# Token-run x loads, taps as shifts by 32 columns, GELU in store order: a causal convolution and an MLP on one core

## The chip, the cores and the metric

The kernel runs on one core of a Trainium2 chip. The metric is the device time of one execution in microseconds, and each median below is over several executions on one chip. The batches of experiments ran on different chips, each with the kernel before beside it, so a run is compared with the kernel before of its own batch. The span in the profile is 1.7 to 2.2 us shorter than the time of the same execution.

Names: PE is the TensorE matmul, PEld its weight load, DVE is VectorE, ACT is ScalarE, POOL is GpSimd, SP is SyncE. SPq, POOLq and ACTq are the queues on which these engines request DMAs. A load lands when its completion is signalled; an eviction is DVE's copy of a result out of the matmul's buffer; a beat is the time from one GELU tile to the next. The granted clock is the share of TensorE's full speed that the throttle allowed, by the profile's records.

## The reference, cut to what matters

```python
# x: (8, 4096, 192) fp32, weight: (8 heads, 7 taps), w_in: (192, 2048), w_out: (2048, 192)
w = softmax(weight, axis=-1)
x_pad = concat([zeros(B, 6, 192), x], axis=1)          # causal: 6 tokens of halo
out[b, s, h, :] = sum_k w[h, k] * x_pad[b, s + k, head h]
h = out.reshape(32768, 192) @ w_in
y = gelu_exact(h) @ w_out                              # (32768, 192) fp32
```

## The kernel before

The 32768 tokens are cut into two halves that are worked on side by side, on partitions 0 to 63 and 64 to 127. A block is 512 tokens of each half; the first two blocks are half blocks of 256. For each block, DVE transposes x (three STREAM_TRANSPOSE instructions) and runs 21 tap instructions (7 taps, 3 channel groups); PE multiplies by w_in, ACT applies GELU, PE multiplies by w_out, DVE evicts, SP stores. DVE works one block ahead of PE.

```python
WS = [256, 256] + [512] * ((HALF - 512) // 512)
# POOL: weights requested at once, w_in's second part for one half of the partitions only
for hf in range(2):
    g.dma_start(win[first 512 columns], ...).then_inc(S_WIN[0], 16)
...   # build the head selector
g.dma_start(win[columns 512..2047], ...).then_inc(S_WIN[1], 16)
g.dma_start(wout, ...).then_inc(S_WOUT, 16)
for n in range(1, NB):          # halo: the last 6 tokens of the block before
    ...
    g.tensor_copy(dst, ap(xT[(n - 1) % 2], WS[n - 1], [[NP * XW, 128], [XW, NP], [1, HL]]))
# DVE: tap k reads xT shifted by k columns
src = ap(xT[n % 2], p * XW + k, [[NP * XW, 128], [1, w]])
# SP: x in pieces of 160 floats (640 bytes), one piece for each token
ap(xt, off, [[D, 32], [32 * D, w // 32], [1, XC]])
# SP at the start
load(0)
sp.wait_ge(S_XIN[0], 64)
load(1)
sp.wait_ge(S_WIN[1], 16)
sp.dma_start(win[other partitions], win[...])   # copy of w_in's second part inside SBUF
load(2)
for n in range(1, NB + 1):
    if n + 2 < NB: load(n + 2)
    if n >= 2: store(n - 2, 1)
    store(n - 1, 0)             # each block is stored in two halves
store(NB - 1, 1)
```

I call the x of blocks 0, 1, 2 and 3 x0, x1, x2 and x3.

## Time and profile before

The median is 704.16 us in the first three runs.

| quantity | value | read from |
|---|---|---|
| PE busy from 60 to 690 us | 100%, clock 1.00 | table of stretches |
| one GELU tile on PE (two matmul phases) | 1.31 us | timeline |
| GELU on ACT | 1.024 us | groups |
| first matmul of block 2 | 43.66 us | timeline |
| end of the last eviction to the end of the span | 3.0 us | timeline |

The first view is the timeline of the start-up: start, duration, engine, line, operation and, in brackets, the idle time before it and what ended that. A merged row such as the x requests shows its first start and its total extent.

```profile
0.81 10.27 SPq L406 DMA_DIRECT2D xin<-in_x_dram  x8
4.30 0.65 POOL L146 DMA_DIRECT2D win<-in_moe_w_in_dram  x1
9.35 1.10 DVE L193 STREAM_TRANSPOSE xT<-xin 128x256 f32<-128x256 f32 x3 [3.34 <-DMA xin<-in_x_dram]
12.07 0.70 SPq L431 DMA_DIRECT2D win<-win  x1
12.81 13.91 SPq L406 DMA_DIRECT2D xin<-in_x_dram  x8
28.38 1.90 DVE L193 STREAM_TRANSPOSE xT<-xin 128x512 f32<-128x512 f32 x3 [0.40 <-DMA xin<-in_x_dram]
30.32 1.28 DVE L214 TENSOR_SCALAR acc<-xT,wcol 128x512 f32<-128x512 f32 x3
43.66 0.82 PE L333 MATMUL hp<-xc,win 64*128 64x512 bf16 x6 [4.02 <-DVE xc L221]
```

DVE starts when x0 has landed (9.35 us) and waits only 0.40 us for x2 at 28.38 us. PE starts block 2 at 43.66 us, held by DVE's taps. From then on PE sets the pace, so a delay at this point is a delay of the whole kernel, to within about 2 us: in the twelve kernels of the table further down, the stretch from this matmul to the end of the last eviction took 654.9 to 657.5 us.

The table of stretches: window and length, busy time and count of PE, PEld, DVE, ACT and POOL, granted clock, DMA share, GB/s. The DMA share is the mean busy share of the 16 DMA engines; packets that overlap on one engine make it exceed 1.

```profile
7.00:13.00 6.00, 0.00 (x0) 0.00 (x0) 3.62 (x11) 0.00 (x0) 0.20 (x1) 1.00 1.24 192
13.00:19.00 6.00, 0.39 (x5) 0.35 (x7) 5.66 (x15) 0.00 (x0) 0.00 (x0) 1.00 1.24 234
19.00:25.00 6.00, 5.92 (x59) 4.06 (x54) 5.96 (x17) 3.85 (x4) 0.31 (x1) 1.00 1.18 198
```

DVE, once it has x0, waits only 0.34 and 0.40 us for x.

The groups of instructions by shape (total busy us, mean ns, idle before, releaser), before:

```profile
L289 ACT ACTIVATE gT<-hp 128x1024 bf16<-128x1024 f32 x512 | 523.6, 1024 | 161.2 <-PE hp L333 161.2
L214 DVE TENSOR_SCALAR acc<-xT,wcol 128x512 f32<-128x512 f32 x93 | 39.6, 482 | 1.1
L162 POOL COPY xT<-xT 128x18 f32<-128x18 f32 x29 | 12.6, 436 | 567.9 <-DVE xT L193 567.9
```

The middle of the kernel in the view of stretches, and the end of the timeline; the span is 702.9 us:

```profile
60.00:690.00 630.00, 630.00 (x10615) 480.59 (x10612) 497.43 (x817) 493.52 (x482) 11.58 (x28) 1.00 0.47 98
```

```profile
689.38 10.93 SPq L418 DMA_DIRECT2D out_dram<-osb  x3
699.35 0.56 DVE L230 COPY osb<-ob 128x384 f32<-128x384 f32 x1 [0.76 <-PE ob L365]
```

### The profile page before, as it was taken

What the parts mean: (1) busy time and instruction counts of PE and PEld (TensorE: products, weight loads), DVE (VectorE), ACT (ScalarE), POOL (GpSimd) and SP (SyncE); (2) the same over time, 40 slices, a digit from 0 to 9 for tenths busy, and PEclk for the clock granted to TensorE, in tenths of its full rate; (3) what the DMA queues carried; (4) which work ended last, traced back from release to release, by engine and by line L of the source; (5) the groups of instructions that cost most, each with busy time, mean ns of one, the idle gap of its engine ahead of it and who ended that gap; (6) DMA issues with size and microseconds to landing.
All of it is one profiled execution on the core that took longest, in us unless ns stands there. A gap on an engine that the chain in (4) does not pass through costs nothing.

```text
span 702.9 us, 24699 instructions
## 1 busy us (share of the span) xinstructions
PE 676.9 (96%) x11366; PEld 518.1 (74%) x11366; DVE 550.2 (78%) x925; ACT 526.5 (75%) x516; POOL 17.9 (3%) x44
## 2 busy tenths in 40 slices
PE   0879999999999999999999999999999999999997
PEld 0657777777777777777777777777777777777777
DVE  5999778977777977777987777887777897777711
ACT  1669777777777777777777777777777777777771
POOL 2000000000000000000000000000000000000000
PEclk9999999999999999999999999999999999999999
DMA  9945555335555335555434555434565533551012
GB/s 183 177 92 106 123 115 101 84 81 108 123 121 98 91 79 99 122 121 99 101 84 82 122 122 100 108 83 75 121 123 115 100 86 79 108 121 48 24 47 70
DMA packets 104487, 71.05 MB, mean 101 GB/s; under 512 B 5312, under 2 KB 104000, under 8 KB 104384
## 3 DMA queue, kind: packets, MB, share of 16 engines
q1 hardware_dynamic: 101680, 67.71, 46.3%
q0 software_dynamic: 2688, 1.77, 1.8%
q8 instruction: 89, 1.46, 0.9%
q14 instruction: 14, 0.11, 0.1%
q10 hardware_dynamic: 16, 0.00, 0.0%
HBM read 45.48 MB, written 25.17 MB: 101 GB/s over the span
## 4 chain that ended last, share of the span: by engine, by line
PE 93%; DMA 3%; DVE 2%; SPq 0%; issue 0%; POOL 0%; POOLq 0%
PE ob L365 47%; PE hp L333 46%; DMA xin<-in_x_dram 2%; DVE acc L221 1%; DMA win<-in_moe_w_in_dram 1%; SPq L406 0%; POOL win L117 0%; DVE xT L193 0%; DVE acc L214 0%; DVE xc L221 0%; SPq L431 0%; DVE osb L230 0%; POOL sel L124 0%; POOL sel L134 0%; POOL sel L121 0%
## 5 line engine op out<-in xcount | busy, mean ns | idle before, releaser
L289 ACT ACTIVATE gT<-hp 128x1024 bf16<-128x1024 f32 x512 | 523.6, 1024 | 161.2 <-PE hp L333 161.2
L365 PEld LDWEIGHTS ob<-wout,gT 64*128 64x128 bf16 x8192 | 368.9, 94 | 103.2 <-issue 0.7
L333 PE MATMUL hp<-xc,win 64*128 64x512 bf16 (+1 forms) x3168 | 426.9, 373 | 18.1 <-DVE xc L221 16.8
L365 PE MATMUL ob<-wout,gT 64*128 64x192 bf16 x8192 | 428.9, 243 | 0.0
L221 DVE SCALAR_TENSOR_TENSOR acc<-xT,wcol,acc 128x512 f32<-128x512 f32 (+1 forms) x495 | 327.4, 730 | 0.0
L333 PEld LDWEIGHTS hp<-xc,win 64*128 64x128 bf16 x3168 | 163.1, 95 | 73.4 <-issue 18.5
L230 DVE COPY osb<-ob 128x384 f32<-128x384 f32 x128 | 71.0, 556 | 139.3 <-PE ob L365 139.3
L221 DVE SCALAR_TENSOR_TENSOR xc<-xT,wcol,acc 128x512 bf16<-128x512 f32 (+1 forms) x99 | 66.8, 730 | 0.0
L193 DVE STREAM_TRANSPOSE xT<-xin 128x512 f32<-128x512 f32 (+1 forms) x99 | 60.8, 665 | 4.1 <-DMA xin<-in_x_dram 4.1
L214 DVE TENSOR_SCALAR acc<-xT,wcol 128x512 f32<-128x512 f32 (+1 forms) x99 | 41.4, 474 | 1.2
L162 POOL COPY xT<-xT 128x18 f32<-128x18 f32 x29 | 12.6, 436 | 567.9 <-DVE xT L193 567.9
L304 PE MATMUL ob<-wnm,sel 8*128 8x7 f32 x6 | 1.4, 358 | 4.4 <-POOL sel L134 4.4
L304 PEld LDWEIGHTS ob<-wnm,sel 8*128 8x128 f32 x6 | 1.3, 320 | 4.4 <-POOL sel L134 4.4
L274 ACT ACT_TABLE_LOAD x1 | 1.3, 1283 | 1.4 <-PEq L458 1.4
L170 DVE TENSOR_REDUCE wmx<-wsb 8x1 f32<-8x7 f32 x1 | 0.1, 148 | 2.2 <-DMA wsb<-in_weight_dram 2.2
L182 DVE COPY wcol<-ob 128x21 f32<-128x21 f32 x1 | 0.2, 181 | 2.1 <-PE ob L304 2.1
L159 POOL MEMSET xT<- 128x18 f32 x3 | 0.3, 115 | 41.9 <-DVE xc L221 41.9
L117 POOL DMA_DIRECT2D win<-in_moe_w_in_dram x2 | 1.4, 688 | 0.8 <-POOLq L458 0.8
L289 ACT ACT_TABLE_LOAD x1 | 1.3, 1283 | 0.0
L150 POOL DMA_DIRECT2D wout<-in_moe_w_out_dram x1 | 1.2, 1194 | 0.0
L174 DVE TENSOR_SCALAR wsm<-wsm 8x1 f32<-8x1 f32 x1 | 0.1, 142 | 0.8 <-ACT wex L274 0.8
L146 POOL DMA_DIRECT2D win<-in_moe_w_in_dram x1 | 0.6, 647 | 0.0
(12 smaller groups left out, 2.8 us busy)
## 6 DMA issues: line engine op xcount, KB each, us to landing
xin<-in_x_dram SPq DMA_DIRECT2D x124, 320.0 KB, 6.6
out_dram<-osb SPq DMA_DIRECT2D x62, 384.0 KB, 3.0
xin<-in_x_dram SPq DMA_DIRECT2D x8, 160.0 KB, 6.1
wout<-in_moe_w_out_dram POOLq DMA_DIRECT2D x1, 768.0 KB, 17.1
out_dram<-osb SPq DMA_DIRECT2D x4, 192.0 KB, 5.0
win<-in_moe_w_in_dram POOLq DMA_DIRECT2D x1, 576.0 KB, 7.7
win<-win SPq DMA_DIRECT2D x1, 576.0 KB, 9.2
win<-in_moe_w_in_dram POOLq DMA_DIRECT2D x2, 192.0 KB, 6.1
```

Source lines behind the costliest of these rows:

```text
L117: g.dma_start(ap(win, 64 * hf * NP * F, [[NP * F, 64], [F, NP], [1, FC]]), ap(wint, 0, [[F, 64], [64 * F, NP], [1, FC]]),).then_inc(S_WIN[ ...
L150: g.dma_start(ap(wout, 0, [[NF * C, 128], [C, NF], [1, C]]), ap(woutt, 0, [[C, 128], [128 * C, NF], [1, C]]),).then_inc(S_WOUT, 16)
L162: g.tensor_copy(dst, ap(xT[(n - 1) % 2], WS[n - 1], [[NP * XW, 128], [XW, NP], [1, HL]]),).then_inc(S_HALO)
L193: v.transpose(ap(xT[n % 2], p * XW + HL, [[NP * XW, 128], [1, w]]), ap(xin[n % NX], 64 * p, [[TB // 32 * XC, 128], [XC, w // 32], [1, 32]] ...
L214: ins = v.tensor_scalar(a, src, wk, None, ALU.mult)
L221: ins = v.scalar_tensor_tensor(dst, src, wk, a, op0=ALU.mult, op1=ALU.add)
L230: v.tensor_copy(ap(osb[m % 2], 2 * g * C, [[8 * C, 128], [C, 2], [1, C]]), ap(ob[(G0[m] + g) % 2], 0, [[1024, 128], [512, 2], [1, C]]),).t ...
L274: a.activation(out=wex[:, :], in_=wsb[:, :], func=AF.Exp, bias=wmx[:, 0:1], accum_out=wsm[:, 0:1],).then_inc(S_ACTP)
L289: a.activation(out=ap(gT[n % 2], i * c * 2 * w, [[NF * 2 * TB, 128], [w, 2], [2 * w, c], [1, w]],), in_=hp[u % 2][:, :], func=AF.Gelu,).th ...
L304: ins = t.matmul(ob[0][:, p * KS : (p + 1) * KS], sel[:, p * 128 : (p + 1) * 128], wnm[:, :],)
L333: ins = t.matmul(hp[u % 2][:, hf * TB + cc * w : hf * TB + cc * w + w], win[r, p * F + f0 : p * F + f0 + 128], xc[n % 2][r, p * TB : p * T ...
L365: ins = t.matmul(ob[gg % 2][:, 512 * sub : 512 * sub + C], gT[m % 2][r, c0 : c0 + 128], wout[r, i * C : (i + 1) * C], start=(ph == 0 and i ...
```

## The change

The intent is that each partition holds a run of 16 consecutive tokens. One load descriptor is then 12 KB instead of 640 bytes. After the transpose, neighbouring tokens lie 32 columns apart, so a tap is a shift by 32 columns. The halo is no longer 6 columns but 6 x 32: 31 of each 32 columns are copied from the same block, on GpSimd (558 elements per partition), and one of 32 from the block before. GELU writes its output in an order in which each partition of the result holds 4 consecutive tokens, so a store descriptor is 3 KB instead of 768 bytes. The change also holds the weights back until x0 and x1 have landed, and stores a block whole with four DMAs.

```diff
-    HL = KS - 1
+    HB = KS - 1
+    HL = 32 * HB
...
-            for hf in range(2):                      # w_in, first part, at once
-                g.dma_start(... ).then_inc(S_WIN[0], 16)
             g.memset(sel[:, :], 1.0).then_inc(S_SEL)
...
+            def halo(n):
+                ...   # 18 elements from the block before (or zeros)
+                g.wait_ge(S_TR, NP * (n + 1))
+                g.tensor_copy(
+                    ap(xT[n % 2], 1, [[NP * XW, 128], [XW, NP], [32, HB], [1, 31]]),
+                    ap(xT[n % 2], WS[n], [[NP * XW, 128], [XW, NP], [32, HB], [1, 31]]),
+                ).then_inc(S_HALO)
+            g.wait_ge(S_XIN[0], 64)
+            for hf in range(2):
+                g.dma_start(... ).then_inc(S_WIN[0], 16)
+            halo(0)
+            g.wait_ge(S_XIN[1], 64)
             g.dma_start(...).then_inc(S_WIN[1], 16)  # w_in, second part
             g.dma_start(...).then_inc(S_WOUT, 16)
...
-                    v.wait_ge(S_HALO, n + 1)
+                if k == 1 and p == 0:
+                    v.wait_ge(S_HALO, 2 * n + 2)
...
-                src = ap(xT[n % 2], p * XW + k, [[NP * XW, 128], [1, w]])
+                src = ap(xT[n % 2], p * XW + 32 * kt, [[NP * XW, 128], [1, w]])
...
+                    if c == 1:
+                        src = [[2 * TB, 128], [w // 4, 8], [32, w // 128], [1, 32]]
+                        dst = [[NF * 2 * TB, 128], [32, 8], [256, w // 128], [1, 32]]
...
-                        ap(xt, off, [[D, 32], [32 * D, w // 32], [1, XC]]),
+                        ap(xt, off, [[mb * D, 32], [1, mb * D - 32]]),
...
-                if n >= 2:
-                    store(n - 2, 1)
-                store(n - 1, 0)
-            store(NB - 1, 1)
+                store(n - 1)                          # whole, four DMAs
```

More of the change, by code (lines that the diff above doesn't have):

```diff
@@ L37, in bass_lightweight_conv__then__act_gelu_exact_kernel @@
     assert NF == 16
-    XC = 160
-    HL = KS - 1
+    HB = KS - 1
+    HL = 32 * HB
     XW = HL + TB
@@ L55, in bass_lightweight_conv__then__act_gelu_exact_kernel @@
     G0 = [sum(NG[:n]) for n in range(NB + 1)]
+    OUTS = []
+    for n in range(NB):
+        OUTS.append((64 if NCH[n] == 1 else 128) + (OUTS[n - 2] if n >= 2 else 0))
     es = ExitStack()
@@ L81, in bass_lightweight_conv__then__act_gelu_exact_kernel @@
         wcol = sbt("wcol", [128, NP * KS], F32)
-        xin = [sbt("xin%d" % i, [128, TB // 32 * XC], F32) for i in range(NX)]
+        xin = [sbt("xin%d" % i, [128, TB // 32 * D], F32) for i in range(NX)]
         xT = [sbt("xT%d" % i, [128, NP * XW], F32) for i in range(2)]
@@ L115, in _ @@
         def _(g):
-            for hf in range(2):
-                g.dma_start(
-                    ap(win, 64 * hf * NP * F, [[NP * F, 64], [F, NP], [1, FC]]),
-                    ap(wint, 0, [[F, 64], [64 * F, NP], [1, FC]]),
-                ).then_inc(S_WIN[0], 16)
             g.memset(sel[:, :], 1.0).then_inc(S_SEL)
@@ L142, in _ @@
             ).then_inc(S_SEL)
-            halo_memset = ap(xT[0], 0, [[NP * XW, 128], [XW, NP], [1, HL]])
-            g.memset(halo_memset, 0.0).then_inc(S_HALO)
+            def halo(n):
+                dst = ap(xT[n % 2], 0, [[NP * XW, 128], [XW, NP], [32, HB]])
+                if n >= 2:
+                    g.wait_ge(S_CV, NCV * (n - 1))
+                if OFF[n] % SEQ == 0:
+                    g.memset(dst, 0.0).then_inc(S_HALO)
+                else:
+                    g.wait_ge(S_TR, NP * n)
+                    g.tensor_copy(
+                        dst,
+                        ap(
+                            xT[(n - 1) % 2],
+                            WS[n - 1] + 31,
+                            [[NP * XW, 128], [XW, NP], [32, HB]],
+                        ),
+                    ).then_inc(S_HALO)
+                g.wait_ge(S_TR, NP * (n + 1))
+                g.tensor_copy(
+                    ap(xT[n % 2], 1, [[NP * XW, 128], [XW, NP], [32, HB], [1, 31]]),
+                    ap(xT[n % 2], WS[n], [[NP * XW, 128], [XW, NP], [32, HB], [1, 31]]),
+                ).then_inc(S_HALO)
+            g.wait_ge(S_XIN[0], 64)
+            for hf in range(2):
+                g.dma_start(
+                    ap(win, 64 * hf * NP * F, [[NP * F, 64], [F, NP], [1, FC]]),
+                    ap(wint, 0, [[F, 64], [64 * F, NP], [1, FC]]),
+                ).then_inc(S_WIN[0], 16)
+            halo(0)
+            g.wait_ge(S_XIN[1], 64)
             g.dma_start(
@@ L154, in _ @@
             for n in range(1, NB):
-                dst = ap(xT[n % 2], 0, [[NP * XW, 128], [XW, NP], [1, HL]])
-                if n >= 2:
-                    g.wait_ge(S_CV, NCV * (n - 1))
-                if OFF[n] % SEQ == 0:
-                    g.memset(dst, 0.0).then_inc(S_HALO)
-                else:
-                    g.wait_ge(S_TR, NP * n)
-                    g.tensor_copy(
-                        dst,
-                        ap(xT[(n - 1) % 2], WS[n - 1], [[NP * XW, 128], [XW, NP], [1, HL]]),
-                    ).then_inc(S_HALO)
+                halo(n)
         @block.vector
@@ L191, in trans @@
                     if n >= 1:
-                        v.wait_ge(S_HALO, n)
+                        v.wait_ge(S_HALO, 2 * n)
                 v.transpose(
@@ L197, in trans @@
                         64 * p,
-                        [[TB // 32 * XC, 128], [XC, w // 32], [1, 32]],
+                        [[TB // 32 * D, 128], [D, w // 32], [1, 32]],
                     ),
@@ L205, in conv @@
                     v.wait_ge(S_TR, NP * (n + 1))
-                    v.wait_ge(S_HALO, n + 1)
+                if k == 1 and p == 0:
+                    v.wait_ge(S_HALO, 2 * n + 2)
                 idx = NCV * n + NP * k + p
+                kt = KS - 1 - k
                 if idx >= NP:
                     v.wait_ge(S_CV, idx - NP + 1)
-                src = ap(xT[n % 2], p * XW + k, [[NP * XW, 128], [1, w]])
-                wk = wcol[:, p * KS + k : p * KS + k + 1]
+                src = ap(xT[n % 2], p * XW + 32 * kt, [[NP * XW, 128], [1, w]])
+                wk = wcol[:, p * KS + kt : p * KS + kt + 1]
                 a = acc[:, p * TB : p * TB + w]
@@ L228, in evac @@
                 if m >= 2 and g == 0:
-                    v.wait_ge(S_OUT[m % 2], 32 * (m // 2))
+                    v.wait_ge(S_OUT[m % 2], OUTS[m - 2])
                 v.tensor_copy(
-                    ap(osb[m % 2], 2 * g * C, [[8 * C, 128], [C, 2], [1, C]]),
+                    ap(osb[m % 2], g * C, [[8 * C, 128], [4 * C, 2], [1, C]]),
                     ap(ob[(G0[m] + g) % 2], 0, [[1024, 128], [512, 2], [1, C]]),
@@ L288, in _ @@
                         a.wait_ge(S_MM2, G0[n - 1])
-                    a.activation(
-                        out=ap(
-                            gT[n % 2],
-                            i * c * 2 * w,
-                            [[NF * 2 * TB, 128], [w, 2], [2 * w, c], [1, w]],
-                        ),
-                        in_=hp[u % 2][:, :],
+                    if c == 1:
+                        src = [[2 * TB, 128], [w // 4, 8], [32, w // 128], [1, 32]]
+                        dst = [[NF * 2 * TB, 128], [32, 8], [256, w // 128], [1, 32]]
+                    else:
+                        src = [[2 * TB, 128], [TB, 2], [128, 4], [1, 128]]
+                        dst = [[NF * 2 * TB, 128], [128, 2], [256, 4], [1, 128]]
+                    a.activation(
+                        out=ap(gT[n % 2], i * c * 2 * w, dst),
+                        in_=ap(hp[u % 2], 0, src),
                         func=AF.Gelu,
@@ L400, in load @@
             def load(n):
-                w = WS[n]
+                mb = WS[n] // 32
                 if n >= NX:
@@ L408, in load, with store @@
                             xin[n % NX],
-                            32 * q * (TB // 32 * XC),
-                            [[TB // 32 * XC, 32], [XC, w // 32], [1, XC]],
+                            32 * q * (TB // 32 * D),
+                            [[TB // 32 * D, 32], [1, mb * D - 32]],
                         ),
-                        ap(xt, off, [[D, 32], [32 * D, w // 32], [1, XC]]),
+                        ap(xt, off, [[mb * D, 32], [1, mb * D - 32]]),
                     ).then_inc(S_XIN[n % NX], 16)
-            def store(m, hf):
+            def store(m):
@@ L416, in store @@
                 w = WS[m]
-                sp.wait_ge(S_EV, G0[m] + (NG[m] if hf else (NG[m] + 1) // 2))
-                sp.dma_start(
-                    ap(outt, (hf * HALF + OFF[m]) * C, [[C, 128], [128 * C, w // 128], [1, C]]),
-                    ap(
-                        osb[m % 2],
-                        hf * (w // 128) * C,
-                        [[8 * C, 128], [C, w // 128], [1, C]],
-                    ),
-                ).then_inc(S_OUT[m % 2], 16)
+                j = w // 128
@@ new lines, in store @@
+                mb = w // 32
+                sp.wait_ge(S_EV, G0[m + 1])
+                for q in range(4):
+                    if NCH[m] == 1:
+                        dst = ap(
+                            outt,
+                            (OFF[m] + j * q) * C,
+                            [[mb * C, 32], [HALF * C, 2], [1, j * C]],
+                        )
+                        src = ap(
+                            osb[m % 2],
+                            32 * q * 8 * C,
+                            [[8 * C, 32], [4 * C, 2], [1, j * C]],
+                        )
+                        sp.dma_start(dst, src).then_inc(S_OUT[m % 2], 16)
+                    else:
+                        assert j == 2
+                        for b in range(2):
+                            dst = ap(
+                                outt,
+                                (OFF[m] + 4 * b + q) * C,
+                                [[mb * C, 32], [HALF * C, 2], [1, C]],
+                            )
+                            src = ap(
+                                osb[m % 2],
+                                32 * q * 8 * C + b * C,
+                                [[8 * C, 32], [4 * C, 2], [1, C]],
+                            )
+                            sp.dma_start(dst, src).then_inc(S_OUT[m % 2], 16)
@@ L438, in _ @@
                     load(n + 2)
-                if n >= 2:
-                    store(n - 2, 1)
-                store(n - 1, 0)
-            store(NB - 1, 1)
+                store(n - 1)
             for s in range(2):
-                sp.wait_ge(S_OUT[s], 32 * ((NB + 1 - s) // 2))
+                sp.wait_ge(S_OUT[s], OUTS[NB - 1 if (NB - 1) % 2 == s else NB - 2])
 _INS = ['x', 'weight', 'moe_w_in', 'moe_w_out']
```

## The prediction

> **What bounds the kernel now.** TensorE. The table of stretches shows PE 100% busy at full clock from 60 to 690 us; the timeline shows a beat of 1.31 us per GELU tile (0.65 us for the first matmul, 0.66 for the second). From 61.6 us, where the beat settles, to the last matmul at 699.3 us PE waits for nothing. ACT needs 1.024 us of each beat; DVE idles 139 us waiting for PE (about 3.6 us per block of 20.9 us); DMA moves 101 GB/s on average. Only two pieces can move: the start-up (61.6 us, limited by DVE) and the tail (3.6 us; the last store takes 3.0 us from issue to landing).
>
> **Start-up, by the timeline.** DVE starts block 0's transpose at 9.35 us, when the first x load (640-byte packets, competing with the weights) has landed. It then works nearly without a gap until 43.5 us: about 9.3 us for each of the two half blocks, 15.2 us for block 2, one wait of 0.4 us for x. PE starts block 2 at 43.66 us after idling 4.0 us, then runs at a granted clock of 0.66 for 5 us.
>
> **What changes there.** 12 KB runs (6 KB in the half blocks), with the weights held back until x is in: I estimate x for block 0 at about 5.4 us, from the 3.0 us of a 384 KB store, so DVE starts 4 us earlier. The second part of w_in is requested at about 10.5 us (4.3 before), its copy done at about 21 us (21.4 before), so PE should be no later in block 0. x for block 2 should land near 25 us (28.4 before).
>
> **What it costs.** The halo copy on GpSimd grows from 18 to 558 elements plus the 18, and taps 1 to 6 wait for it. The 18-element copies took 0.20, 0.31 and 0.45 us against 0.1 us for an 18-element memset: they stand behind one tensor_scalar (0.3 or 0.43 us). The Trainium skill, "SBUF — State Buffer", section "Who interferes with whom", calls this an exclusive lock of the shared port pair; the trace agrees. I estimate 0.6 to 1.0 us for the large copy (384 elements took 0.41 to 0.54 us), lost to DVE once per block: about 3 us over four start-up blocks, nothing afterwards, because it fits into DVE's 3.6 us of idle time. Net start-up gain about 2 us.
>
> The tail loses: the last block is stored whole after the last eviction, 768 KB in four DMAs, instead of a last half of 384 KB: +1.5 us by four issues of about 0.45 us at 300 GB/s.
>
> GELU in store order writes runs of 32 elements. The Trainium skill, "ScalarE: Activation LUTs", gives one element per cycle whatever the function; I expect 1.02 us still. Taps stay at about 0.67 us.
>
> **Predicted: 703.6 us, 80% range 701.0 to 707.0. Faster by over 2%: 0.01; within 2%: 0.95; slower by over 2%: 0.04.**
>
> **What would show it.** First transpose at 5 to 6.5 us; large copy 0.6 to 1.0 us and a DVE gap of about 0.7 us per block before tap 1; block 2's first matmul at 41 to 43 us; beat still 1.31 us; GELU 1.02 us; last eviction to end of span 4 to 5 us instead of 3.0.
>
> **What would make it wrong.** GELU above 1.3 us (PE would wait for ACT in every beat); a GpSimd copy above 4 us (DVE would become the limit); the w_in copy landing after 27 us (PE late in block 0).

## The result, and the profile after

The changed kernel takes 713.48 us (713.05 to 714.92, 4 runs) against 704.51 us (703.26 to 705.44, 4 runs) before. The ratio is 1.0132, with a 95% interval of 1.0110 to 1.0154. A ratio here is the mean time of one kernel's runs over that of the other's in the same rounds, so it isn't quite the ratio of the medians. The loss of 9 us is real. At 1.3% it is within the 2% to which the prediction gave 0.95, but 713.48 lies outside the range of 701.0 to 707.0.

The start-up after, in the same view:

```profile
0.82 7.07 SPq L434 DMA_DIRECT2D xin<-in_x_dram  x8
6.26 1.10 DVE L215 STREAM_TRANSPOSE xT<-xin 128x256 f32<-128x256 f32 x3 [0.74 <-DMA xin<-in_x_dram]
13.81 0.63 POOL L178 DMA_DIRECT2D win<-in_moe_w_in_dram  x1 [5.28 <-DMA xin<-in_x_dram]
20.10 0.70 SPq L482 DMA_DIRECT2D win<-win  x1
20.84 5.25 SPq L434 DMA_DIRECT2D xin<-in_x_dram  x8
27.72 6.04 PE L361 MATMUL hp<-xc,win 64*128 64x256 bf16 x60 [8.54 <-DMA win<-win]
34.91 1.90 DVE L215 STREAM_TRANSPOSE xT<-xin 128x512 f32<-128x512 f32 x3 [9.06 <-DMA xin<-in_x_dram]
36.85 1.75 DVE L238 TENSOR_SCALAR acc<-xT,wcol 128x512 f32<-128x512 f32 x3
50.66 1.47 PE L361 MATMUL hp<-xc,win 64*128 64x512 bf16 x6 [3.67 <-DVE xc L245]
```

DVE does start 3.1 us earlier (6.26 against 9.35). But w_in's second part is requested at 13.81 us instead of 4.30, because POOL waits for x1. SP waits for that part to land before it requests the copy inside SBUF (20.10 instead of 12.07), and x2 is requested behind the copy (20.84 instead of 12.81). x2 lands at 34.9 us; DVE has waited 9.06 us for it. From its first request to its landing x2 took 14.1 us, against 15.6 before (12.81 to 28.38): it is late because it is requested late, not because it moves more slowly. Block 2's first matmul comes at 50.66 us instead of 43.66, that is 7.0 us later: 6.53 us by the later start of the transposes (34.91 against 28.38) and 0.47 us by the tensor_scalars (1.75 against 1.28).

SP's own waits say the same. First before, then after:

```profile
SPq L431 <- DMA win<-in_moe_w_in_dram: 1.0, 1, 1.0
```

```profile
SPq L482 <- DMA win<-in_moe_w_in_dram: 12.2, 1, 12.2
```

The three stretches after:

```profile
7.00:13.00 6.00, 0.00 (x0) 0.00 (x0) 5.96 (x15) 0.00 (x0) 1.53 (x4) 1.00 0.90 192
13.00:19.00 6.00, 2.56 (x24) 1.92 (x24) 5.96 (x16) 1.02 (x1) 3.47 (x5) 1.00 0.67 98
19.00:25.00 6.00, 0.18 (x2) 0.00 (x0) 6.00 (x17) 1.02 (x1) 0.00 (x0) 0.82 1.41 204
```

From 13 to 19 us the DMA engines move 98 GB/s instead of 234, at a share of 0.67: they stand partly idle while one request waits for another load's landing, and the bytes that they could have moved have to be moved later. The share alone is no rate: from 7 to 13 us 192 GB/s went with 1.24 before and with 0.90 after.

The groups after. GELU is unchanged to the nanosecond. The small POOL copy has its large companion, and the mean tensor_scalar grew from 482 to 636 ns, although it computes the same:

```profile
L321 ACT ACTIVATE gT<-hp 128x1024 bf16<-128x1024 f32 x512 | 523.5, 1024 | 167.9 <-PE hp L361 167.9
L238 DVE TENSOR_SCALAR acc<-xT,wcol 128x512 f32<-128x512 f32 x93 | 54.3, 636 | 1.1
L164 POOL COPY xT<-xT 128x558 f32<-128x558 f32 x33 | 21.6, 653 | 609.2 <-DVE xT L215 609.2
```

The middle and the end after; the span is 711.7 us:

```profile
60.00:690.00 630.00, 630.00 (x10586) 473.43 (x10582) 514.68 (x827) 495.40 (x485) 28.21 (x57) 1.00 0.49 110
```

```profile
696.08 12.69 SPq L461 DMA_DIRECT2D out_dram<-osb  x8
706.05 0.56 DVE L254 COPY osb<-ob 128x384 f32<-128x384 f32 x1 [0.76 <-PE ob L393]
```

The last eviction ends at 706.61 us, 6.7 us later than before (699.91), and 5.1 us follow it instead of 3.0. These two are the whole loss of span: 6.7 + 2.1 = 8.8 us = 711.7 - 702.9. Between 60 and 690 us nothing was lost: PE is 100% busy at clock 1.00 in both kernels.

### The profile page after: what moved, and what is told of

It reads as the page before. It is cut to its first block, busy times and chain, and to the rows that moved or that the text cites. A ratio compares the mean times of both kernels' runs of the same rounds, so it can differ in the third digit from the quotient of the medians. Undisturbed runs are those within 1.5% of the kernel's fastest.

```text
span 711.7 us, 24838 instructions
## 1 busy us (share of the span) xinstructions
PE 677.3 (95%) x11366; PEld 511.9 (72%) x11366; DVE 563.4 (79%) x925; ACT 526.4 (74%) x516; POOL 37.4 (5%) x77
## 4 chain that ended last, share of the span: by engine, by line
PE 92%; DMA 4%; DVE 2%; SPq 1%; issue 0%
PE ob L393 47%; PE hp L361 45%; DMA xin<-in_x_dram 3%; DVE acc L245 1%; DMA win<-in_moe_w_in_dram 1%; SPq L434 1%; DVE acc L238 0%; DVE xT L215 0%; DVE xc L245 0%; SPq L482 0%; DVE osb L254 0%
## 5 line engine op out<-in xcount | busy, mean ns | idle before, releaser
L393 PEld LDWEIGHTS ob<-wout,gT 64*128 64x128 bf16 x8192 | 364.4, 94 | 107.3 <-issue 0.5
L361 PEld LDWEIGHTS hp<-xc,win 64*128 64x128 bf16 x3168 | 159.2, 95 | 82.8 <-issue 26.1
L238 DVE TENSOR_SCALAR acc<-xT,wcol 128x512 f32<-128x512 f32 (+1 forms) x99 | 57.5, 632 | 1.2
L164 POOL COPY xT<-xT 128x558 f32<-128x558 f32 x33 | 21.6, 653 | 609.2 <-DVE xT L215 609.2
## 6 DMA issues: line engine op xcount, KB each, us to landing
wout<-in_moe_w_out_dram POOLq DMA_DIRECT2D x1, 768.0 KB, 10.5
```

What stands on the lines that cost most here:

```text
L164: g.tensor_copy(ap(xT[n % 2], 1, [[NP * XW, 128], [XW, NP], [32, HB], [1, 31]]), ap(xT[n % 2], WS[n], [[NP * XW, 128], [XW, NP], [32, HB], ...
L238: ins = v.tensor_scalar(a, src, wk, None, ALU.mult)
L361: ins = t.matmul(hp[u % 2][:, hf * TB + cc * w : hf * TB + cc * w + w], win[r, p * F + f0 : p * F + f0 + 128], xc[n % 2][r, p * TB : p * T ...
L393: ins = t.matmul(ob[gg % 2][:, 512 * sub : 512 * sub + C], gT[m % 2][r, c0 : c0 + 128], wout[r, i * C : (i + 1) * C], start=(ph == 0 and i ...
```

## The experiments

Twelve kernels ran; the table has ten of them, and the two with four half blocks follow in their own section. My theory was that holding the weights back makes a serial chain (HELD). The rivals were that the long loads with more bytes are slow themselves (LOADS) and that the halo copies stall DVE (HALO). A second point was the tail (TAIL). The profiled runs side by side, in us; "copy done" is the request plus the time to landing of the DMA view:

| kernel | median | first transpose | copy of w_in done | x2's transpose | block 2's first matmul | after the last eviction |
|---|---|---|---|---|---|---|
| before | 704.51 | 9.35 | 21.3 | 28.38 | 43.66 | 3.0 |
| after | 713.48 | 6.26 | 27.6 | 34.91 | 50.66 | 5.1 |
| weights_early | 708.96 | 7.08 | 21.9 | 29.37 | 45.81 | 5.1 |
| before_held | 711.44 | 6.12 | 28.0 | 34.90 | 50.18 | 3.0 |
| second_free | 711.97 | 6.18 | 24.6 | 31.78 | 47.52 | 5.1 |
| short_runs | 714.54 | 6.45 | 29.0 | 36.05 | 51.80 | 5.2 |
| tail_halves | 712.29 | 6.34 | 27.4 | 35.50 | 51.25 | 3.1 |
| halo_18 (wrong) | 712.87 | 6.33 | 27.6 | 34.85 | 50.16 | 5.1 |
| reordered_new | 705.96 | 6.24 | no copy | 27.96 | 46.44 | 3.1 |
| reordered_old | 705.51 | 5.89 | no copy | 27.35 | 45.98 | 3.0 |
| x2_first_old | 705.30 | 8.44 | 20.9 | 30.02 | 45.30 | 3.0 |
| x2_first_new | 704.89 | 7.43 | 26.7 | 26.47 | 44.54 | 3.2 |

The kernel before, run beside each batch, was at 705.32 us (first four), 704.44 us (second four), 704.89 us (the two of four half blocks) and 705.09 us (the last two).

### weights_early: the change without holding the weights back

```diff
+            for hf in range(2):                      # w_in, first part, before the selector
+                g.dma_start(...).then_inc(S_WIN[0], 16)
             g.memset(sel[:, :], 1.0).then_inc(S_SEL)
...
-            g.wait_ge(S_XIN[0], 64)
-            for hf in range(2): g.dma_start(...)
-            halo(0)
-            g.wait_ge(S_XIN[1], 64)
...
-            for n in range(1, NB):
+            for n in range(NB):
                 halo(n)
```

> The changed kernel with the weight loads issued at the start again, as in the kernel before; all else of the change kept. Theory HELD (holding w_in back until x has landed makes a serial chain x1, w_in, copy and x2, and x2 then comes at 34.9 us): x for block 2 lands near 29 to 30 us, block 2's first matmul is at 45 to 46 us instead of 50.7, total 707.5 to 709.5 us. Rival LOADS (12 KB runs with 19% more bytes are themselves the cause of the late x2): block 2's first matmul stays at 49 us or later and the total above 711.5 us. Rival HALO (GpSimd copies stall DVE): no change against 713.5 us.

Measured: 708.96 us (707.32 to 711.15), ratio to before 1.0061 (1.0030 to 1.0091). From its timeline:

```profile
13.85 0.70 SPq L479 DMA_DIRECT2D win<-win  x1
29.37 1.90 DVE L212 STREAM_TRANSPOSE xT<-xin 128x512 f32<-128x512 f32 x3 [3.17 <-DMA xin<-in_x_dram]
33.08 1.46 PE L358 MATMUL hp<-xc,win 64*128 64x256 bf16 x12 [3.83 <-DMA wout<-in_moe_w_out_dram]
45.81 0.81 PE L358 MATMUL hp<-xc,win 64*128 64x512 bf16 x6
```

x2 and block 2 came where HELD put them. About half of the loss is gone. What is left is the tail (2.1 us) and a block 2 that starts 2.15 us later than in the kernel before. Of this, x2 accounts for 1.0 us (29.37 against 28.38) and the tensor_scalars for 0.5 us. The last 0.7 us come from PE, which waited 3.83 us for w_out in block 1 and was not done with block 1 when the taps were: the weights share the DMA engines with x again.

### before_held: the kernel before with nothing but the two waits

```diff
-            for hf in range(2): g.dma_start(...)     # at once
...
+            g.wait_ge(S_XIN[0], 64)
+            for hf in range(2): g.dma_start(...).then_inc(S_WIN[0], 16)
             g.memset(halo_memset, 0.0).then_inc(S_HALO)
+            g.wait_ge(S_XIN[1], 64)
```

> The kernel before with nothing of the change but the two waits: w_in's first part only after x for block 0 has landed, the rest after x for block 1. HELD: the copy of w_in is done at 26 to 28 us, x for block 2 lands at 33 to 35 us, block 2's first matmul at 48 to 50 us, total 708.5 to 711 us. LOADS and HALO: DVE starts earlier and nothing else of the change is there, so 702 to 705 us.

Measured: 711.44 us (709.82 to 712.65), ratio 1.0088 (1.0066 to 1.0109).

```profile
34.90 1.90 DVE L195 STREAM_TRANSPOSE xT<-xin 128x512 f32<-128x512 f32 x3 [9.93 <-DMA xin<-in_x_dram]
50.18 0.82 PE L335 MATMUL hp<-xc,win 64*128 64x512 bf16 x6 [2.86 <-DVE xc L223]
```

The two waits alone, with 640-byte loads, old taps, old halo and old stores, cost 6.1 us (711.44 - 705.32); that is just above my range, as is block 2 (50.18 us). They put x2 at 34.90 us, where the full change has it (34.91). This decides for HELD. It also shows that keeping the weights off the DMA engines is enough for an early first transpose (6.12 us), without the long runs.

### second_free: one of the two waits taken away

```diff
-            g.wait_ge(S_XIN[1], 64)
```

> The changed kernel with one wait less: w_in's second part and w_out no longer wait for x of block 1. HELD: w_in part two is requested at about 8.6 us instead of 13.8, lands at 15 to 16 us instead of 20.1; x2 lands at 28.5 to 30.5 us, block 2's first matmul at 44.5 to 46.5 us, total 706.5 to 709.5 us. LOADS or HALO: within 1.5 us of 713.5 us.

Measured: 711.97 us (711.44 to 712.42), ratio 1.0096 (1.0081 to 1.0112). The direction is HELD's, but the size is a miss. The request moved from 13.81 to 8.38 us, as expected, but the part then took 9.4 us to land instead of 6.3, while w_in's first part and x1 were still on the engines. SP saw it at 17.8 us, only 2.3 us earlier. I had again treated a transfer as if it had the engines to itself. Block 2 started 3.1 us earlier than in the full change, yet the span is only 1.6 us shorter: in the 5 us after that start PE did 34 matmuls at a granted clock of 0.50, against 50 at 0.72.

### short_runs: only the run length undone

```diff
-                            [[TB // 32 * D, 32], [1, mb * D - 32]],
+                            [[TB // 32 * D, 32], [D, mb], [1, 160]],
...
-                        ap(xt, off, [[mb * D, 32], [1, mb * D - 32]]),
+                        ap(xt, off, [[mb * D, 32], [D, mb], [1, 160]]),
```

> The changed kernel with the same token layout and the same waits, but each x load cut into 640-byte pieces as in the kernel before (1.31 MB per block instead of 1.56 MB, 19 times as many descriptors): only the run length differs. HELD: the x loads move about 213 GB/s with 12 KB runs against 182 to 218 GB/s with 640-byte runs, so the bytes saved and the rate lost cancel; x2 lands within 2 us of 34.9 us and the total is within 1.5 us of 713.5 us. LOADS: if long runs with more bytes were the cause, x2 lands before 31 us and the total is under 710.5 us. If long runs are the gain that was intended, it gets slower by over 2 us.

Measured: 714.54 us (714.40 to 714.91), ratio 1.0134 (1.0119 to 1.0149), against 1.0132 for the full change. In the stretch from 28 to 35 us it is nearly all x that moves (in short_runs the copy landed only at 29.0). First the full change with 12 KB runs, then this kernel:

```profile
28.00:35.00 7.00, 6.59 (x72) 4.16 (x68) 0.09 (x1) 4.99 (x5) 0.00 (x0) 0.64 1.01 217
```

```profile
28.00:35.00 7.00, 5.87 (x56) 3.90 (x58) 0.00 (x0) 3.58 (x4) 0.00 (x0) 1.00 1.23 195
```

The long runs move 217 GB/s and the short ones 195: 11% more, on loads that carry 19% more bytes (380 KB against 320 KB for each DMA). LOADS falls, and so does the hope that far fewer descriptors would bring a clear gain here. (They are 16 times fewer for a full block, since 16 pieces of 640 bytes stand for each run; the 19 of the expectation divides the run's 12 KB by 640 bytes.) The two ratios differ by 0.0002, with intervals that leave room for about 2 us either way. The Trainium skill ("Perfetto Trace Analysis", section "DMA Optimizations") says that small DMAs, under 2 KB, carry a significant overhead and that batching them "can dramatically improve throughput". Here each DMA is 320 KB or more and only its runs are short, which is not quite the page's case; it shows 11%.

### tail_halves: the last block stored in two parts

```diff
+            store_last(sp, 0, range(4))     # after the second eviction, runs of 2 tokens
+            store_last(sp, 1, range(2))     # after the fourth; ACT issues the other two
```

> The changed kernel, but the last block alone is stored in two parts (after the second and after the fourth eviction, runs of 2 tokens), and two of the last four DMAs are issued by ACT. Theory TAIL (2.1 us of the loss lie after the last eviction, because one whole block of 768 KB is stored there by four DMAs in a row): last eviction's end to the end of the span 3.0 to 3.8 us instead of 5.1 us, total 711.5 to 712.5 us instead of 713.5. If the start-up were all of it, no change.

Measured: 712.29 us (711.91 to 713.76), ratio 1.0113 (1.0097 to 1.0129). 3.1 us follow the last eviction instead of 5.1. In its profiled run block 2 happened to start 0.6 us later than in the full change's, so compare the stage, not the totals: storing the last block whole costs 2.0 us.

### halo_18: the large halo copy cut to 18 elements

```diff
-                    ap(xT[n % 2], 1, [..., [32, HB], [1, 31]]),
+                    ap(xT[n % 2], 1, [..., [32, HB], [1, 1]]),     # and its source; halo zeroed once
```

> The changed kernel with the large halo copy cut from 558 to 18 elements (wrong result on purpose). Theory LOCK (the copy holds the port pair that the tensor_scalar wants): the three tensor_scalars of a 512-wide block take 1.28 us again instead of 1.75, DVE gains about 0.5 us per block; since DVE's waits for x2 hide the first two blocks, block 2's first matmul moves by 0.5 us only and the total by 0.3 to 1.0 us. Rival HALO (the halo copies are the main loss): the total falls by over 3 us.

The result was wrong (relative error 0.44). Measured: 712.87 us (2 runs), ratio 1.0117 (1.0095 to 1.0140). The tensor_scalars of block 2:

```profile
36.78 1.31 DVE L242 TENSOR_SCALAR acc<-xT,wcol 128x512 f32<-128x512 f32 x3
```

They take 1.31 us, against 1.75 with the large copy and 1.28 before. So the copy costs DVE about 0.45 us per block, by standing in the way of an instruction that doesn't depend on it, and block 2 moves by 0.5 us. In the full change the first of the three tensor_scalars takes all of it: 958 ns in block 2, against about 470 for the other two and 523 for the first here. The Trainium skill ("SBUF — State Buffer", section "Who interferes with whom") describes this as a port pair that whoever comes first holds for the whole instruction. The trace agrees that the one is held up until the other ends: the copy ends at 37.53 us and that tensor_scalar 0.28 us later. It doesn't show who came first, since by the profile the tensor_scalar began 0.03 us before the copy (36.85 and 36.88). HALO as the main cause falls: the total is 0.6 us under the full change's, in another round, and not by over 3 us.

### reordered_new and reordered_old: the loads in order of need

```diff
-            g.dma_start(win second part, one half of the partitions)     # and a copy by SP later
+            for hf in range(2): g.dma_start(win second part, half hf)    # both from DRAM, no copy
+            g.wait_ge(S_XA, 32)                                          # half of x2 has landed
             g.dma_start(wout, ...)
...
             load(2)
+            sp.wait_ge(S_WOUT, 16)                                       # then x3
```

A first form of both kernels waited for half of the count of x2's own semaphore. Later increments could satisfy it too; a semaphore of its own (S_XA) mended it.

The edit does less than the expectation says. Both kernels kept SP's wait for w_in's second part (its first half) in front of the request for x2, though x2 doesn't need it. SP stood there for 10.0 us in reordered_new and 10.5 us in reordered_old, so this order of loads was never tried without that wait.

> The changed kernel with the start-up loads ordered by need and none waiting for a landing that it doesn't depend on: x0, then w_in's first part, x1, both halves of w_in's second part straight from DRAM (no copy inside the chip), x2, w_out after half of x2, x3 after w_out; and the last block stored in two parts. Theory ENGINE TIME (before x2, all loads together need about 28 us of the 16 DMA engines, so only the order and the gaps matter): first transpose at 6.2 us, x2 lands at 25 to 28 us, block 2's first matmul at 42 to 44.5 us, total 702 to 706 us. If x2 still lands after 31 us, the total stays above 708 us.

> The same order of loads in the kernel before (its own layout, halo and stores unchanged). ENGINE TIME: first transpose at 6.1 us, x2 lands at 24 to 27 us, block 2's first matmul at 41 to 43.5 us, total 701 to 704.5 us; against reordered_new it is 0.5 to 2.5 us faster, because DVE has no stall by the large halo copies and x is 16% smaller per block.

Measured: 705.96 us (ratio 1.0016, 0.9999 to 1.0033) and 705.51 us (1.0011, 0.9996 to 1.0027). x2 landed at 27.96 us, within its range, and at 27.35, just above it; DVE still waited 2.13 and 2.34 us for it. The total of reordered_new is within its range, that of reordered_old 1.0 us above. Block 2 missed in both: it began at 46.44 us and not by 44.5, and at 45.98 us and not by 43.5. DVE had block 2's taps done by about 43.5 and 42.4 us, so it was PE that was late. What I took away from x2 came back as a wait for w_out, 5.69 us in reordered_new and 4.92 us in reordered_old:

```profile
33.50 1.46 PE L384 MATMUL hp<-xc,win 64*128 64x256 bf16 x12 [5.69 <-DMA wout<-in_moe_w_out_dram]
```

### four_small_old and four_small_new: four half blocks at the start

```diff
-    WS = [256, 256] + [512] * ((HALF - 512) // 512)
+    WS = [256] * 4 + [512] * ((HALF - 1024) // 512)
```

> The kernel before with one line changed: four half blocks of 256 columns at the start instead of two. If the start-up is what can move (DVE's taps and x for the first 512-wide block hold PE back), then x for block 2 is half as large and its taps take about 9.3 us instead of 17, so block 2's first matmul is at 37.5 to 40.5 us instead of 43.7, PE has no gap of 4 us before it, and the total is 698.5 to 702 us. If only the last stages count, no change.

> The same four half blocks in the changed kernel with the weights issued at the start and the last block stored in two parts. Block 2's first matmul at 38 to 41.5 us, total 700 to 704 us: within 2.5 us of four_small_old, slower rather than faster, because of the halo copies and the longer x loads.

Both missed: 706.68 us (ratio 1.0022, 1.0009 to 1.0035) and 711.44 us (1.0098, 1.0079 to 1.0116). In the old layout block 2 did begin early, at 38.56 us and without a gap. But PE needs only 10.5 us for a half block, and DVE needs 15.3 us and more for the first full one, so the gap moved to block 4 and grew. From the timeline of four_small_old:

```profile
65.04 1.46 PE L333 MATMUL hp<-xc,win 64*128 64x512 bf16 x6 [5.26 <-DVE xc L221]
```

In the new layout the same gap was 9.99 us, with a wait of 4.17 us for x in front of it.

### x2_first_old and x2_first_new: x2 no longer behind the copy

```diff
-            sp.wait_ge(S_WIN[1], 16)
-            sp.dma_start(win other half <- win).then_inc(S_WIN[2], 16)
             load(2)
+            sp.wait_ge(S_XIN[2], 64)                                     # then x3
...
+            a.wait_ge(S_WIN[1], 16)                                      # ACT issues the copy
+            a.dma_start(win other half <- win).then_inc(S_WIN[2], 16)
```

x2_first_new has this on top of weights_early and tail_halves.

> The kernel before, with the copy of w_in issued by ACT so that x2 no longer queues behind it and its wait, and with x3 requested only when x2 has landed. ENGINE TIME: x2 is limited by what the 16 DMA engines have to move before it, so taking x3 and half of the copy away from it should bring it from 28.4 us to 25 to 27 us; DVE then has no wait, block 2's first matmul is at 41.5 to 43 us, total 701.5 to 704 us. If x2 stays at 28 us or later, the total stays within 1 us of the kernel before.

> The same in the changed kernel, with the weights issued at the start and the last block stored in two parts. x2 at 26 to 28.5 us (29.4 in weights_early), block 2's first matmul at 43 to 45.5 us, total 703 to 707 us: this would undo the gating and the tail and leave the halo copies and the 19% larger x loads, 0.5 to 3 us above x2_first_old.

Measured: 705.30 us (ratio 1.0008, 0.9994 to 1.0023) and 704.89 us (1.0012, 0.9989 to 1.0035; one of its six runs took 710.16 us, and I can't say why). The new layout is within its ranges, except that it is not slower than the old one. The old layout missed its range: x1 now came at 20.97 us and made DVE wait 3.37 us, where before it had waited 0.34. In the new layout:

```profile
26.47 1.88 DVE L212 STREAM_TRANSPOSE xT<-xin 128x512 f32<-128x512 f32 x3
26.86 4.83 PE L381 MATMUL hp<-xc,win 64*128 64x256 bf16 x48 [6.98 <-DMA win<-win]
44.54 0.83 PE L381 MATMUL hp<-xc,win 64*128 64x512 bf16 x6
44.76 0.56 DVE L251 COPY osb<-ob 128x384 f32<-128x384 f32 x1 [2.23 <-PE ob L413]
```

x2 is there without a wait; the copy is now late (PE waits 6.98 us for it), and this time it is PE that sets block 2's start: DVE was done with its taps at about 42.0 us and then waited 2.23 us for PE. So the change, with its order of loads and its last store repaired, ties with the kernel before. No version that I tried is faster than the kernel before.

The Trainium skill ("DMA: Bandwidth & Descriptors", section "Issuing engines are not separate DMA queues") says that DMAs run on the same 16 engines whichever engine requests them. These runs fit that: requested by ACT, the copy took 9.2 us to land in x2_first_old, as it did when SP requested it before, and each reordering took time from one load and gave it to another (x1, x2, w_out or the copy), and block 2 began between 44.5 and 46.4 us in all four, never before 43.66.

## Why the prediction was wrong

**What held.** PE bounds the kernel, the beat stayed, and only the start-up and the tail moved. GELU stayed at 1.024 us. The first transpose at 6.26 us lies in the predicted 5 to 6.5. The large halo copy took 0.65 us (predicted 0.6 to 1.0) and cost DVE 0.45 to 0.47 us per full block (predicted about 0.7), though not where I expected it: there is no gap before tap 1, the first instruction of tap 0 is stretched. The tail lost 2.1 us (predicted 1.5).

**What failed.** The step that failed is "The second part of w_in is requested at about 10.5 us (4.3 before), its copy done at about 21 us", together with "x for block 2 should land near 25 us". Measured: requested at 13.81, copy done at 27.6, x2 landed at 34.9 us. With these I had forecast a start-up gain of 2 us; it was a loss of 7.0 us. The prediction did name the late copy of w_in (after 27 us) among the things that would make it wrong, but not the late x2, which was the one that counted.

**The error behind it.** The prediction moved w_in's second part back by 6 us, from 4.3 to 10.5, and x2 forward by 3 us. It left out a wait that both kernels have: SP requests the copy only when that part has landed, and x2 only behind the copy. The profile before has what this wait costs. From the request of the part to the first request of x2 went 8.5 us (4.30 to 12.81), and from there to x2's landing 15.6 us (12.81 to 28.38). With the predicted request at 10.5 us this puts x2 at 34.6 us, not 25; measured were 13.81, 20.84 and 34.91. The request itself came 3.3 us later than predicted, because x1 landed about 6 us after its last request, while w_in's first part was on the engines too; the part and the copy then landed somewhat faster than before (6.3 and 7.5 us, against 7.7 and 9.2). The prediction does not say how it came to 21 and 25 us; the one landing time that it names is that of a 384 KB store (3.0 us), and it uses it for x0.

before_held shows that this chain alone costs 6.1 of the 9.0 us. The tail adds 2.0 to 2.1 us and the halo copy about 0.5 us. The three come from different rounds and add up to 8.6 to 8.7 us.

**The attribution of the gain.** I credited the early x0 to "12 KB runs (6 KB in the half blocks), with the weights held back". Either of the two does most of it alone. The first transpose came at 9.35 us with neither, at 7.08 with long runs alone (weights_early), at 6.12 and 6.45 with held weights alone (before_held, short_runs), and at 6.26 with both; each is one profiled run. So the waits, which cost 6.1 us, brought x0 only 0.8 us more than the long runs alone. The lines that would have warned me were there before I predicted: a DMA share above 1 from 7 to 25 us. Where the engines are busy throughout, holding one load back doesn't remove it, and here each wait on a landing also left them partly idle (0.67 from 13 to 19 us).

**What stays open.** How much of the remaining start-up is unavoidable is not settled: no order that I tried started a full block 2 before 43.66 us, which isn't proof that none can; in reordered_old DVE had the taps done at 42.4 us, and only PE's wait for w_out was in the way. Why single runs of weights_early and x2_first_new were 2 to 5 us longer is not explained either; they have the lowest granted clocks of their kernels (0.991 against 0.993 to 0.995, and 0.997 against 1.000), which goes with the length but is not shown to cause it.

## What to carry to other kernels

Before you move a request, follow every later request back through the waits in front of it, and put your own predicted times into that chain. Look at the DMA share and rate of the start-up by themselves, not at the average over the span: where the engines are busy throughout, count all loads that must come before the critical one, and treat a wait on one landing before the next request as a hole. A load that is held back to favour another one should wait only for what it needs, and nothing else should queue behind it on the same issuing engine. At the end of a kernel, store in parts as the parts become ready.

## What the Trainium skill lacked or had wrong

- "Perfetto Trace Analysis", section "DMA Optimizations", says that batching small DMAs, under 2 KB, can improve throughput dramatically; it doesn't say what short runs inside a large DMA cost. Here 640-byte against 12 KB runs gave 195 against 217 GB/s in the same stretch and no gain in the total that the runs resolve. Only where the weights were on the engines too did x0 gain clearly: the first transpose came at 7.08 us with 6 KB runs and at 9.35 with 640-byte runs.
- "DMA: Bandwidth & Descriptors" gives a fit for the time of one DMA. It lacks a warning, with a number, that landing times don't carry over to a busy start-up: w_in's second part took 6.3 us to land in the changed kernel, 9.4 us in second_free and 11.3 us in four_small_new, with the same bytes.
- "TensorE: Matmul & The Clock Gate", Part 1, says that the clock events in a trace have been seen to be unreliable, and has no such pair of traces as this one: after 8.5 and 9.4 us without a matmul, the changed kernel and before_held both ran their first GELU tiles at a beat of 1.26 to 1.30 us and both did 72 matmuls from 28 to 35 us, but the first has a granted clock of 0.64 there and the second of 1.00.
- No page gives a measured time of a single-input copy on GpSimd by size: 558 fp32 elements per partition took 653 ns, while the adjacent tensor_scalar group lost 0.47 us.
